# A new order of the work list in a fused attention and maxout kernel

## The chip, the cores and the metric

The kernel runs on one core of a Trainium2 chip. The metric is the device time of one execution in microseconds (us). The time before is the median of three runs, 335.35 us (334.3 to 336.46). The profile and the trace come from one profiled execution of the same kernel. Engines are called as in the profile: PE (matmul), PEld (its weight loads), DVE, ACT, POOL and SP.

## The reference

```python
# q, k, v: (8 batches, 12 heads, 448, 64) f32; w1, w2: (768, 1024); w_out: (1024, 768)
scores = scale * q @ k.T                    # scale = 1/8
scores = cap * tanh(scores / cap)           # cap = 30
attn = exp(scores - max) / (sum + 1e-9)     # softmax over the keys
x = (attn @ v)  -> transposed to (3584, 768)
h1 = x @ w1;  h2 = x @ w2
out = maximum(h1, h2) @ w_out               # (3584, 768) f32
```

## The kernel before, in words

**Algebra.** The maximum is written as relu(x @ (w1 - w2)) + x @ w2. So the kernel makes wd = w1 - w2 (step `sub`, six chunks) and wm = w2 @ w_out, which is premultiplied on chip (steps `W` and `WC` turn a chunk of w2 on PE and keep it, `OP` and `P` multiply it by w_out, `PC` keeps the result). Then out = relu(x @ wd) @ w_out + x @ wm. The tanh bounds the scores, so no maximum is subtracted.

**Attention.** The 96 (batch, head) pairs are worked in 24 quads t of four heads; a quad is two pairs i = 2t and 2t+1, and a batch has three quads. For a quad:

- `lk`, `lq` load k and q into one of two buffers `kqs` (POOL's DMA queue, L332 and L339; for pairs from 10 on the k load is two DMAs); `lv` loads v in four parts into `vp` and `vl` (L363, two buffers each).
- For pairs under 10 q and k are transposed on PE (`X`, `Xh`, L462) and kept by DVE (`XC`, `XCh`, L467). From quad 5 on one DMA transpose does it (`cr t`, L479, issued on SP), from `kqs` to one of two buffers `qkT`. So a load into `kqs` for quad t must wait for `cr` t-2, and `cr` t for the last scores of quad t-2.
- `S i j` makes the scores of a pair against 128 keys, for j = 0, 1, 2 (L517); `L t` those of the last 64 keys of all four heads (L531). They alternate between two PSUM slots `s0` and `s1`. ACT takes each with a tanh (`T`, L522; `TL`, L535), and exps follow in place (`E i j0 j1`, `EL`).
- `A` and `B` add the exps up on DVE (L551, L556), `Y` totals them over the keys on PE (L576), `Y1`, `Y2`, `Y3` transpose, invert and spread them (DVE, L581 to L587).
- `VL` and `V` make the values on PE, into one of the same two PSUM slots (L602, L610); `N t u` multiplies by the inverse and frees the slot (DVE, L622, L625). The result is x transposed, `xT`.

**Maxout.** 120 groups of matmuls, 30 for two batches: stage 1 (x @ wd, 448 columns) and stage 2 (relu part @ w_out and x @ wm, 384 columns). They run on four further PSUM banks. `M x y n` issues n pairs: one matmul on the upper 64 rows of the array for group x and one on the lower 64 rows for group y (L649; L644 where x is y). Where a group's bank passes from one half to the other, a hand-over nop carries the dependency: `Hs` on SP (L658), `H` on DVE. `ev` evicts a group on DVE (L670, L706, the last L709), `eva` on ACT (L704), `st` stores 192 KB of the output from SP (L680 to L685), the last two halves from SP and ACT (L711).

**What sets the order.** There is no scheduler at work: a text, `ORDER`, lists every step, and a loop at the end issues them as listed. Each engine (and each DMA queue, which is the issuing engine's own order) runs its instructions in list order; between engines only data, buffers and banks make them wait. `D` steps are matmuls on a constant that keep PE at work while it has nothing else.

```python
for s in ORDER.split(";"):
    if s.strip():
        name, *args = s.split()
        STEPS[name](*[int(a) if a.lstrip("-").isdigit() else a for a in args])
```

Of the kernel before, what the change touches and what calls it, by code (L numbers as in the profile page):

```python
# [9 lines left out]
ld0 k; ld0 q; ms0; lwo 0 0; dm; ms; D 3 27; lw2 2; lk 1 0; id; lq 1 0; cd k; cd q; lw2 0; Xh 0 0 0; lw2 3;  # L10
Xh 0 1; XCh 0 0; lw2 1; D 3 5; XCh 0 1; S 0 0; S 0 1; T 0 0; D 3 16; T 0 1; lq 2 0; S 0 2; D 3 17; lq 3 0;
T 0 2; lk 2 0; X 1 1; E 0 0 3; D 3 14; XC 1; lwo 0 1; L 0; D 3 20; TL 0; lk 3 0; W 3 2; D 3 2; lq 4 0; S 1 0;
WC 3; T 1 0; lv 0 0; W 1 3; EL 0; W 2 0; lv 0 1; WC 1; W 0 1; lv 0 2; WC 2; S 1 1; S 1 2; lv 0 3; T 1 1; WC 0;
X 2 2; lk 4 0; T 1 2; XC 2; OP 0 0 3; P 0 0 4; E 1 0 2; S 2 0; S 2 1; OP 2 0 0; P 2 0 2; lwo 1 0; P 2 0 2;
OP 1 0 1; P 1 0 2; T 2 0; P 1 0 1; lwo 1 1; X 3 2; T 2 1; lk 5 0; P 1 0 1; XC 3; S 2 2; lk 6 0; P 2 0 2; T 2 2;
P 2 0 2; lq 5 0; PC 2 0; E 1 2 3; L 1; lv 1 0; VL 0; V 0 0 0 2; lv 1 1; TL 1; X 4 2; lv 1 2; E 2 0 3;
V 0 1 0 2; XC 4; Y 0 0; V 0 0 2 3; V 0 1 2 3; Y1 0; lv 1 3; S 3 0; OP 2 1 2; P 2 1 1; Y2 0; P 2 1 2; T 3 0;
Y3 0; P 2 1 1; OP 1 1 0; P 1 1 3; N 0 0; P 1 1 1; EL 1; P 1 0 1; S 3 1; N 0 1; P 1 0 2; T 3 1; P 1 0 1; lw2 5;
PC 1 0; S 3 2; S 4 0; lk 7 0; T 3 2; OP 0 1 1; P 0 1 5; lw1 0; E 3 0 2; P 0 1 1; S 4 1; lw1 5; P 0 1 2;
P 0 0 2; PC 0 1; P 0 0 2; P 1 1 1; T 4 0; lq 6 0; P 1 1 1; PC 0 0; X 5 1; lw2 4; T 4 1; S 4 2; XC 5; P 1 1 2;  # L20
lv 2 0; T 4 2; OP 3 0 3; P 3 0 2; PC 1 1; W 5 1; lv 2 1; E 3 2 3; L 2; WC 5; VL 1; lv 2 2; V 1 0 0 2; TL 2;
V 1 1 0 2; Y 1 0; lv 2 3; sub 0 0; E 4 0 3; V 1 0 2 3; V 1 1 2 3; Y1 1; S 5 0; O 0 1; M 0 -1 1; lq 7 0;
P 3 0 2; Y2 1; P 2 1 1; Y3 1; lw1 2; P 2 1 2; T 5 0; X 6 0; lw1 1; N 1 0; P 2 1 1; EL 2; P 3 0 1; N 1 1; S 5 1;
sub 5 1; P 3 0 2; T 5 1; P 3 0 1; XC 6; S 5 2; PC 2 1; T 5 2; W 4 0; PC 3 0; S 6 0; E 5 0 2; WC 4; OP 3 1 2;
P 3 1 1; lk 8 0; X 7 3; lw1 4; S 6 1; XC 7; lq 8 0; P 3 1 2; T 6 0; P 3 1 1; sub 2 0; OP 4 0 0; P 4 0 1;
lk 9 0; P 4 0 3; T 6 1; lq 9 0; P 3 1 1; S 6 2; lq 10 0; P 3 1 2; T 6 2; sub 1 0; P 3 1 1; P 4 0 3; lw1 3;
P 4 0 1; E 5 2 3; L 3; PC 3 1; VL 2; V 2 0 0 2; TL 3; PC 4 0; V 2 1 0 2; lq 11 0; Y 2 3; sub 4 0; E 6 0 3;
lk 10 0; V 2 0 2 3; X 8 2; Y1 2; lk 10 1; V 2 1 2 3; XC 8; S 7 0; lk 11 0; X 9 0; Y2 2; T 7 0; Y3 2; lk 11 1;
M 0 -1 2; EL 3; N 2 0; OP 5 0 3; P 5 0 1; lv 3 0; S 7 1; P 5 0 1; N 2 1; P 5 0 1; T 7 1; P 5 0 1; OP 5 1 2;
P 5 1 1; lv 3 1; P 5 1 3; P 5 0 1; XC 9; lv 3 2; P 5 0 1; S 7 2; S 8 0; A 3 0 1; lv 3 3; T 7 2; P 5 0 2;  # L30
P 5 1 1; A 3 0 2; P 5 1 1; lv 4 0; P 5 1 1; E 7 0 2; P 5 1 1; PC 5 0; S 8 1; lv 4 1; OP 4 1 0; P 4 1 1; PC 5 1;
P 4 1 2; lv 4 2; P 4 1 1; sub 3 0; P 4 1 3; T 8 0; lv 4 3; P 4 1 1; A 3 1 1; lk 12 0; T 8 1; M 0 -1 1; S 8 2;
B 3 0; M 0 -1 1; lk 12 1; M 0 -1 1; T 8 2; O 1 3; M 1 -1 2; B 3 1; Hs 0; cr 5; M 1 -1 1; lq 12 0; M 1 0 1;
E 7 2 3; M 1 0 1; PC 4 1; M 1 0 1; O 2 2; M 2 0 1; L 4; lk 13 0; VL 3; A 3 1 2; TL 4; V 3 0 0 2; lk 13 1;
V 3 1 0 2; Y 3 0; E 8 0 3; V 3 0 2 3; lq 13 0; V 3 1 2 3; Y1 3; S 9 0; M 2 0 2; Y2 3; M 2 1 1; lv 5 0; Y3 3;
M 2 1 2; O 3 0; M 3 1 1; lv 5 1; M 3 1 1; ev 0; Hs 2; M 3 1 1; M 3 2 1; T 9 0; N 3 0; M 3 2 1; lv 5 2; M 3 2 1;
O 4 1; M 4 2 2; EL 4; Hs 3; ev 1; lv 5 3; M 4 2 1; S 9 1; M 4 3 1; N 3 1; lk 14 0; M 4 3 1; T 9 1; M 4 3 1;
O 5 3; M 5 3 2; Hs 4; lk 14 1; M 5 3 1; M 5 4 1; ev 2; M 5 4 1; S 9 2; lq 14 0; S 10 0; ev 3; M 5 4 1; T 9 2;
O 6 2; M 6 4 2; A 4 0 1; Hs 5; M 6 4 1; lk 15 0; M 6 5 1; E 9 0 2; M 6 5 1; ev 4; S 10 1; M 6 5 1; lk 15 1;
O 7 0; M 7 5 1; A 4 0 2; M 7 5 2; Hs 6; M 7 6 1; lq 15 0; M 7 6 1; ev 5; M 7 6 1; T 10 0; O 8 1; M 8 6 1;  # L40
A 4 1 1; M 8 6 1; Hs 7; M 8 6 1; cr 6; M 8 7 1; T 10 1; M 8 7 1; B 4 0; S 10 2; M 8 7 1; O 9 3; M 9 7 1; ev 6;
T 10 2; M 9 7 2; H 8; B 4 1; M 9 8 2; E 9 2 3; M 9 8 2; ev 7; L 5; VL 4; A 4 1 2; TL 5; V 4 0 0 2; V 4 1 0 2;
Y 4 2; E 10 0 3; V 4 0 2 3; V 4 1 2 3; Y1 4; S 11 0; lk 16 0; M 9 8 2; Y2 4; M 9 8 2; Y3 4; lv 6 0; M 9 8 3;
O 10 0; M 10 8 1; N 4 0; lv 6 1; M 10 8 1; Hs 9; M 10 8 1; T 11 0; M 10 9 1; N 4 1; M 10 9 1; Hs 8 2; lv 6 2;
M 10 9 1; M 8 9 2; EL 5; M 8 9 1; lv 6 3; S 11 1; M 8 9 2; A 5 0 1; M 8 9 1; T 11 1; lk 16 1; S 11 2; M 8 9 2;
A 5 0 2; O 11 2; M 11 9 1; lq 16 0; T 11 2; M 11 9 1; S 12 0; ev 8; M 11 9 1; M 11 10 2; ev 9; E 11 0 2;
M 11 10 1; lk 17 0; S 12 1; M 11 10 4; lk 17 1; M 11 10 4; T 12 0; lq 17 0; O 12 1; M 12 10 1; A 5 1 1;
M 12 10 1; Hs 11; cr 7; M 12 10 1; M 12 11 1; B 5 0; M 12 11 1; T 12 1; M 12 11 1; S 12 2; H 10 2; B 5 1;
M 10 11 1; T 12 2; M 10 11 5; E 11 2 3; st 0 0; M 10 11 2; O 13 3; M 13 11 1; ev 10; L 6; VL 5; A 5 1 2; TL 6;
V 5 0 0 2; V 5 1 0 2; Y 5 0; E 12 0 3; V 5 0 2 3; V 5 1 2 3; Y1 5; S 13 0; M 13 11 1; lv 7 0; M 13 11 1; Y2 5;  # L50
M 13 12 2; Y3 5; M 13 12 1; lv 7 1; M 13 12 3; N 5 0; M 13 12 1; lv 7 2; M 13 12 1; T 13 0; M 13 12 1; N 5 1;
M 13 12 1; lv 7 3; M 13 12 1; O 14 0; M 14 12 2; EL 6; Hs 13; S 13 1; lk 18 0; M 14 12 1; M 14 13 1; ev 11;
M 14 13 1; Hs 12 2; T 13 1; S 13 2; lk 18 1; M 14 13 1; A 6 0 1; M 12 13 2; T 13 2; Hs 14; M 12 13 1; lq 18 0;
A 6 0 2; S 14 0; M 12 13 3; E 13 0 2; M 12 13 1; S 14 1; lk 19 0; M 12 13 1; O 15 2; M 15 13 2; ev 12;
M 15 13 1; lk 19 1; M 15 14 2; ev 13; M 15 14 1; T 14 0; O 16 1; M 16 14 1; lq 19 0; A 6 1 1; M 16 14 1;
st 0 1; M 16 14 1; Hs 15; T 14 1; cr 8; B 6 0; M 16 15 1; S 14 2; M 16 15 1; ev 14; M 16 15 1; T 14 2; O 17 3;
M 17 15 2; H 16; M 17 15 1; B 6 1; M 17 16 2; E 13 2 3; M 17 16 1; ev 15; O 18 0; M 18 16 1; L 7; VL 6;
A 6 1 2; st 0 2; TL 7; V 6 0 0 2; V 6 1 0 2; Y 6 2; E 14 0 3; V 6 0 2 3; V 6 1 2 3; Y1 6; S 15 0; M 18 16 1;
lv 8 0; M 18 16 1; Y2 6; M 18 17 1; Y3 6; M 18 17 1; lv 8 1; M 18 17 1; O 19 2; M 19 17 2; ev 16; Hs 18;
lv 8 2; M 19 17 1; M 19 18 1; T 15 0; N 6 0; M 19 18 2; lv 8 3; O 20 1; M 20 18 2; EL 7; Hs 19; ev 17;  # L60
M 20 18 1; lk 20 0; S 15 1; M 20 19 1; N 6 1; M 20 19 1; T 15 1; M 20 19 1; lk 20 1; O 21 3; M 21 19 3; Hs 20;
M 21 20 1; lq 20 0; ev 18; M 21 20 1; S 15 2; S 16 0; ev 19; M 21 20 1; T 15 2; O 22 0; M 22 20 1; lk 21 0;
M 22 20 1; A 7 0 1; Hs 21; M 22 20 1; M 22 21 1; E 15 0 2; M 22 21 1; lk 21 1; ev 20; S 16 1; M 22 21 1;
O 23 2; M 23 21 1; A 7 0 2; M 23 21 1; Hs 22; lq 21 0; M 23 21 1; M 23 22 2; ev 21; M 23 22 1; T 16 0;
M 23 22 2; A 7 1 1; M 23 22 2; cr 9; M 23 22 1; T 16 1; M 23 22 1; B 7 0; S 16 2; M 23 22 2; B 7 1; O 24 1;
M 24 22 1; T 16 2; M 24 22 2; H 23; M 24 23 1; H 22 2; E 15 2 3; M 24 23 2; M 22 23 1; L 8; VL 7; A 7 1 2;
TL 8; V 7 0 0 2; V 7 1 0 2; Y 7 3; E 16 0 3; V 7 0 2 3; lk 22 0; V 7 1 2 3; Y1 7; S 17 0; M 22 23 1; lv 9 0;
M 22 23 1; Y2 7; M 22 23 2; Y3 7; M 22 23 1; lv 9 1; M 22 23 2; O 25 3; M 25 23 1; N 7 0; M 25 23 1; lv 9 2;
M 25 23 1; T 17 0; M 25 24 1; N 7 1; M 25 24 2; lv 9 3; M 25 24 2; EL 8; M 25 24 1; S 17 1; lk 22 1; M 25 24 2;
ev 22; M 25 24 1; T 17 1; S 17 2; lq 22 0; M 25 24 1; ev 23; M 25 24 1; O 26 0; M 26 24 1; T 17 2; M 26 24 1;  # L70
A 8 0 1; Hs 25; S 18 0; M 26 24 1; lk 23 0; M 26 25 1; A 8 0 2; M 26 25 1; Hs 24 2; E 17 0 2; M 26 25 1;
# [145 lines left out]
def kernel(  # L217
# [17 lines left out]
    B, H, S, D = q.shape  # L235
# [3 lines left out]
    P = 128  # L239
    KC, FC = DM // P, DF // P  # L240
    NP = H // 2
    N = B * NP
# [260 lines left out]
    expo = {}  # L503
# [15 lines left out]
    def tanh(i, j):  # L519
        if j == 0:  # L520
            expo[i] = att.tile([P, 2 * NJ, S], bf16, name=f"e{i % 2}")
        nc.scalar.activation(expo[i][:, 2 * j : 2 * j + 2, :], slots[i, j][:, :, :S], AF.Tanh, scale=scale / cap)  # L522
# [260 lines left out]
```

## Time and profile before

| what | before |
|---|---|
| time, median of 3 runs | 335.35 us (334.3 to 336.46) |
| span of the profiled execution | 332.5 us |
| instructions in the trace | 9803 |
| busy: PE, ACT, DVE, POOL | 321.8, 280.8, 240.4, 173.2 us |
| granted PE clock | 1.00 in every stretch |
| start of L602 (values tile) of quad 3, 11, 12, 23 | 60.6, 154.3, 165.7, 292.6 us |

The span is the time from the first to the last instruction of one execution; 2.85 us lie between it and the median of the runs. The busy time of an engine is what its instructions took; a PE that is busy is not therefore at its peak, since matmuls overlap. A row of a timeline gives start, length, engine, line, operation, what it writes and reads, and in brackets how long the engine had been idle and what ended that. The start of the first L602 of each quad is a good clock for progress, since there is one a quad.

### The profile page before, as it was taken

The page shows a single profiled execution, that of the slowest core. Times are in us where ns is not written, and L with a number is a line of the kernel's source. Part 1 is how long each engine was busy: PE and PEld are TensorE (multiplying, and loading weights), DVE is VectorE, ACT ScalarE, POOL GpSimd, SP SyncE. Part 2 cuts the span into 40 slices and gives each one's busy share as a digit, 9 for nine tenths or more (in the row PEclk, how much of TensorE's full clock was granted, in tenths as well). Part 3 has the DMA queues.
Part 4 walks back from the last instruction along what each step waited for, and adds up shares of the span by engine and source line. Part 5 has one row for each costly group of instructions (what it writes and reads, how often), then busy time and mean ns, then how long its engine had stood idle before and what let it go on. Part 6 is the DMA issues. An engine that isn't in the chain of part 4 may idle for free.

```text
span 332.5 us, 9803 instructions
## 1 busy us (share of the span) xinstructions
PE 321.8 (97%) x4139; PEld 183.9 (55%) x4140; DVE 240.4 (72%) x421; ACT 280.8 (84%) x276; POOL 173.2 (52%) x256
## 2 busy tenths in 40 slices
PE   7799998999999999999999999999999999999995
PEld 3444453455556655655656664556566556557662
DVE  2236879898788787986997788978888879973201
ACT  4799997999999999999999999999999999931120
POOL 6586698855775654746783582586456502000000
PEclk9999999999999999999999999999999999999999
DMA  7999999997999999999999999999997973013033
GB/s 137 190 155 184 231 229 135 104 141 71 162 194 188 83 209 140 166 100 164 173 175 95 164 169 170 141 92 194 177 139 71 225 168 45 3 49 97 0 97 95
DMA packets 136044, 45.89 MB, mean 138 GB/s; under 512 B 116417, under 2 KB 131009, under 8 KB 136001
## 3 DMA queue, kind: packets, MB, share of 16 engines
q0 software_dynamic: 96416, 25.08, 76.9%
q1 hardware_dynamic: 39280, 19.77, 30.6%
q8 instruction: 32, 0.52, 0.6%
q10 hardware_dynamic: 304, 0.43, 0.4%
q14 instruction: 12, 0.09, 0.1%
HBM read 47.45 MB, written 11.01 MB: 176 GB/s over the span
## 4 chain that ended last, share of the span: by engine, by line
PE 84%; DMA 8%; DVE 5%; issue 1%; POOL 1%; DVEq 0%; POOLq 0%
PE mm L649 60%; PE s L610 8%; PE s L517 8%; DMA osb<-in_moe_w_dram 2%; DMA gT<-in_moe_w_dram 2%; DMA xT<-in_moe_w_dram 2%; PE s L531 2%; DMA wo_sb<-in_moe_w_out_dram 2%; PE mm L576 2%; PE mm L644 1%; PE s L602 1%; DVE wd_sb L406 1%; PE mm L435 1%; DVE xT L625 1%; DVE wm_sb L441 1%
## 5 line engine op out<-in xcount | busy, mean ns | idle before, releaser
L522 ACT ACTIVATE e<-s 128x896 bf16<-128x896 f32 x144 | 125.5, 923 | 11.1 <-PE s L517 10.8
L539 ACT ACTIVATE e<-e 128x2688 bf16<-128x2688 bf16 (+2 forms) x72 | 122.6, 1704 | 0.0
L649 PE MATMUL mm<-wo_sb,gT 64*128 64x384 bf16 x864 | 115.1, 323 | 0.0
L649 PE MATMUL mm<-wm_sb,xT 64*128 64x384 bf16 x648 | 102.0, 322 | 0.0
L649 PE MATMUL mm<-xT,wd_sb 64*128 64x448 bf16 x768 | 96.7, 349 | 0.7 <-DVE wd_sb L406 0.6
L339 POOL DMA_DIRECT2D kqs<-in_k_dram x76 | 54.8, 723 | 63.8 <-DMA qkT<-kqs 63.2
L649 PEld LDWEIGHTS <-gT 64*128 64x128 bf16 x864 | 58.3, 94 | 25.7 <-issue 0.7
L649 PEld LDWEIGHTS <-wd_sb 64*128 64x128 bf16 x768 | 49.0, 94 | 26.9 <-DVE wd_sb L406 1.3
L649 PEld LDWEIGHTS <-xT 64*128 64x128 bf16 x648 | 50.6, 94 | 18.8
L517 PE MATMUL s<-qkT 64*128 64x448 bf16 x288 | 52.0, 353 | 2.0 <-DVE xT L625 1.7
L670 DVE TENSOR_SCALAR gT<-mm 128x448 bf16<-128x448 f32 x64 | 38.9, 618 | 8.8 <-PE mm L649 7.7
L363 POOL DMA_DIRECT2D vp<-in_v_dram x48 | 30.5, 642 | 22.0 <-PE s L517 21.5
L610 PE MATMUL s<-e,vp 128*32 128x448 bf16 x576 | 36.7, 354 | 0.0
L339 POOL DMA_DIRECT2D kqs<-in_q_dram x38 | 35.2, 926 | 1.0 <-DMA vp<-in_v_dram 1.0
L551 DVE TENSOR_TENSOR esum<-e 128x896 bf16<-128x896 bf16 x42 | 26.0, 619 | 9.7 <-ACT e L539 9.6
L363 POOL DMA_DIRECT2D vl<-in_v_dram x48 | 29.3, 617 | 5.9 <-DMA osb<-in_moe_w_dram 2.4
L517 PEld LDWEIGHTS <-qkT 64*128 64x128 bf16 x288 | 18.5, 94 | 23.1 <-issue 15.0
L625 DVE TENSOR_TENSOR xT<-s,inv 64x448 bf16<-64x448 f32 x48 | 29.9, 622 | 0.9
L551 DVE TENSOR_TENSOR esum<-esum,e 128x896 bf16<-128x896 bf16 x42 | 26.2, 624 | 5.8 <-ACT e L539 4.8
L704 ACT COPY osb<-mm 128x384 f32<-128x384 f32 x10 | 4.8, 479 | 26.9 <-PE mm L649 26.7
L706 DVE COPY osb<-mm 128x384 f32<-128x384 f32 x44 | 23.3, 553 | 5.1 <-PE mm L649 4.6
L556 DVE TENSOR_TENSOR esum<-esum,el 64x896 bf16<-64x896 bf16 x42 | 26.0, 619 | 1.2
(58 smaller groups left out, 266.6 us busy)
## 6 DMA issues: line engine op xcount, KB each, us to landing
out_dram<-osb SPq DMA_DIRECT2D x54, 192.0 KB, 4.8
vp<-in_v_dram POOLq DMA_DIRECT2D x38, 160.0 KB, 4.3
kqs<-in_q_dram POOLq DMA_DIRECT2D x47, 112.0 KB, 6.0
kqs<-in_k_dram POOLq DMA_DIRECT2D x76, 56.0 KB, 4.0
wo_sb<-in_moe_w_out_dram POOLq DMA_DIRECT2D x4, 384.0 KB, 6.6
osb<-in_moe_w_dram POOLq DMA_DIRECT2D x2, 512.0 KB, 5.6
osb<-in_moe_w_dram POOLq DMA_DIRECT2D x4, 256.0 KB, 6.6
kqs<-in_k_dram POOLq DMA_DIRECT2D x9, 112.0 KB, 6.6
```

The costliest lines, as they stand in the source:

```text
L339: nc.gpsimd.dma_start(out=to, in_=x)
L363: nc.gpsimd.dma_start(out=to, in_=x)
L517: nc.tensor.matmul(s[:, h, :S], k_of(t, o, h, j), q_of(t, o, h))
L522: nc.scalar.activation(expo[i][:, 2 * j : 2 * j + 2, :], slots[i, j][:, :, :S], AF.Tanh, scale=scale / cap)
L539: nc.scalar.activation(e, e, AF.Exp, scale=float(cap))
L551: nc.vector.tensor_add(d, e[:, 0:2, :] if j == 1 else d, e[:, 2 * j : 2 * j + 2, :])
L556: nc.vector.tensor_add(d, d, left_e[t][r, :, :])
L610: nc.tensor.matmul(vals[t][place(m, u), u, :S], w[:, m, :], expo[2 * t + o][:, 2 * j + h, :], start=False, stop=(j == NJ - 1))
L625: nc.vector.tensor_mul(x[r : r + 64], vals[t][r : r + 64, u, :S], sums[t, 3][64 - r : 128 - r])
L649: ins = nc.tensor.matmul(self.ps, w[r], x[r], start=first, stop=self.at == [self.n, self.n]).ins
L670: nc.vector.tensor_relu(gT[b // 2][:, f, cs], ps)
L706: nc.vector.tensor_copy(o[:, hs], ps)
```

## The change

The whole list is replaced by another one. Every kind of step occurs as often as before, with the same tiles and buffers, but for the hand-overs: 108 `Hs` and 23 `H` in place of 107 and 21. Runs of single `M` steps are joined (1985 entries in place of 2399). What moves:

- In front, w2's chunk 3 leads the POOL queue and w_out's first half comes behind four chunks of w2; the scores of a pair need not begin with j = 0 any more, which is what the edit in `tanh` allows.
- Loads are listed in bursts, in which those of two or three quads are mixed. Below, the loads and transposes of quads 15 to 17 are shown from both lists.
- `N` of a quad often stands behind two or three evictions on DVE; `Hs` stands directly behind `cr` in several places.
- At the end three stores stand together behind the last `eva`, and groups 118 and 119 alternate.

```diff
-ld0 k; ld0 q; ms0; lwo 0 0; dm; ms; D 3 27; lw2 2; lk 1 0; id; lq 1 0; cd k; cd q; lw2 0; Xh 0 0 0; lw2 3;
-Xh 0 1; XCh 0 0; lw2 1; D 3 5; XCh 0 1; S 0 0; S 0 1; T 0 0; D 3 16; T 0 1; lq 2 0; S 0 2; D 3 17; lq 3 0;
-T 0 2; lk 2 0; X 1 1; E 0 0 3; D 3 14; XC 1; lwo 0 1; L 0; D 3 20; TL 0; lk 3 0; W 3 2; D 3 2; lq 4 0; S 1 0;
...
-M 55 54 1; T 29 1; S 29 2; lq 34 0; M 55 54 1; ev 53; M 55 54 1; O 56 0; M 56 54 1; T 29 2; M 56 54 1;
-A 14 0 1; Hs 55; S 30 0; M 56 54 1; lk 35 0; M 56 55 1; A 14 0 2; M 56 55 1; Hs 54 2; E 29 0 2; M 56 55 1;
-S 30 1; lk 35 1; M 54 55 1; Hs 56; M 54 55 4; lq 35 0; M 54 55 3; T 30 0; O 57 1; M 57 55 1; A 14 1 1;
-M 57 55 1; cr 16; M 57 55 1; M 57 56 1; ev 54; M 57 56 1; T 30 1; M 57 56 1; S 30 2; ev 55; M 57 56 2; T 30 2;
...
-M 117 116 2; eva 115; M 117 116 5; st 7 4; M 117 116 4; M -1 116 2; Hs 117; M -1 116 1; M -1 117 2; Hs 116 2;
-M -1 117 1; M 116 117 8; M -1 117 2; eva 116; M -1 117 1; O 118 1; M 118 118 1; eva 117; M 118 118 6; st 7 5;
-M 118 118 7; O 119 3; M 119 119 2; ev 118; M 119 119 12; ev 119; st 7 6;
+ld0 k; ld0 q; dm; ms0; ms; cd k; id; lw2 3; lq 1 0; lk 1 0; lw2 0; lw2 2; lw2 1; lk 2 0; lq 2 0; lwo 0 0; lk 3 0;
+lq 3 0; lwo 0 1; D 3 8; cd q; D 3 24; Xh 0 0 0; Xh 0 1; D 3 4; XCh 0 0; XCh 0 1; D 3 4; S 0 1; D 3 4; W 3 2;
+S 0 0; X 1 1; T 0 1; T 0 0; WC 3; XC 1; S 0 2; L 0; D 3 28; W 2 0; D 3 4; T 0 2; E 0 0 3; TL 0; D 3 7; S 1 2;
...
+M 50 48 3; S 27 1; Hs 49; ev 47; N 12 0; ev 48; N 12 1; T 27 1; M 50 49 3; Hs 50; lk 30 0; lq 31 0; lq 30 0;
+lv 13 2; lk 32 1; lk 30 1; lv 13 0; lk 33 0; lk 31 0; lk 31 1; lv 13 3; lk 33 1; lv 14 3; lv 13 1; O 51 2;
...
+T 28 0; E 27 2 3; Hs 51; M 52 51 3; O 53 1; M 53 51 3; Hs 52; cr 15; A 13 0 2; ev 50; ev 51; M 53 52 3; S 28 1;
...
+ev 53; lv 15 3; lv 14 0; lq 33 0; lk 34 0; lv 14 1; lk 35 0; lq 35 0; lv 14 2; lq 32 0; lk 32 0; T 29 0;
...
+T 29 2; T 30 0; st 2 1; Hs 55; Hs 54 2; M 56 55 3; M 54 55 6; S 30 1; M 54 55 2; O 57 1; M 57 55 3; Hs 56; cr 16;
...
+Hs 116; st 6 2; M 114 115 6; O 117 2; M 117 115 2; eva 114; M 117 115 1; M 117 116 11; Hs 117; M -1 116 3;
+M -1 117 2; Hs 116 2; M -1 117 1; M 116 117 8; M -1 117 3; eva 115; eva 116; eva 117; st 7 4; st 7 5; st 7 3;
+O 118 1; M 118 118 4; O 119 3; M 119 119 4; M 118 118 10; M 119 119 6; ev 118; M 119 119 4; ev 119; st 7 6;
...
     def tanh(i, j):
-        if j == 0:
+        if i not in expo:
             expo[i] = att.tile([P, 2 * NJ, S], bf16, name=f"e{i % 2}")
         nc.scalar.activation(expo[i][:, 2 * j : 2 * j + 2, :], slots[i, j][:, :, :S], AF.Tanh, scale=scale / cap)
```

## The prediction

> **What bounds the kernel now.** First the page's busy shares, then its chain, then windows, then the timeline of one period. The columns of the windows are: time, sum, PE, PEld, DVE, ACT, POOL, granted clock, DMA share, GB/s.
>
> ```profile
> PE 321.8 (97%) x4139; PEld 183.9 (55%) x4140; DVE 240.4 (72%) x421; ACT 280.8 (84%) x276; POOL 173.2 (52%) x256
> ...
> 0.00:10.00 10.00, 7.33 (x51) 2.86 (x52) 1.84 (x9) 5.17 (x6) 6.00 (x15) 1.00 0.85 147
> 10.00:20.00 10.00, 8.72 (x125) 4.87 (x126) 3.83 (x6) 7.59 (x8) 6.42 (x12) 1.00 1.23 185
> ...
> 50.00:60.00 10.00, 8.62 (x80) 4.31 (x78) 9.69 (x18) 8.29 (x10) 8.53 (x13) 1.00 1.25 119
> 140.00:160.00 20.00, 20.00 (x276) 11.42 (x273) 16.41 (x30) 19.72 (x20) 12.31 (x19) 1.00 1.31 135
> ```
>
> The windows show two regimes. In the first 60 us PE is idle 6.7 us (the 10 us windows sum to 53.3 busy) and ACT some 12. From 60 to 320 PE has no gap, and ACT is at 19.0 to 19.9 of every 20 us until 280. The chain, in order of time (start, us, what), says the same:
>
> ```profile
> 1.26 6.20 DMA wo_sb<-in_moe_w_out_dram
> 7.75 7.10 DMA gT<-in_moe_w_dram
> ...
> 38.84 7.24 DMA osb<-in_moe_w_dram
> 46.07 0.81 issue
> 46.88 1.23 DVE wd_sb L406
> ...
> 323.81 4.67 PE mm L644 x28
> ```
>
> Until 58 us it runs through weight loads and DVE, then through PE alone to 328.5, an eviction and the last stores. One period (one quad of four heads, t) is what to price. In the timeline (start, us, engine, line), left-over scores L531 start at 154.12, their tanh L535 at 154.58, the values tile L602 at 154.32; the next L602 is at 165.73:
>
> ```profile
> 154.12 0.38 PE L531 MATMUL s<-qkT 64*32 64x448 bf16 x8
> 154.32 0.37 PE L602 MATMUL s<-el,vl 64*32 64x448 bf16 x8
> 154.58 0.92 ACT L535 ACTIVATE el<-s 128x896 bf16<-128x896 f32 x1 [0.22 <-PE s L531]
> 155.80 0.65 DVE L581 STREAM_TRANSPOSE st<-mm 128x448 f32<-128x448 f32 x1 [0.53 <-PE mm L576]
> ...
> 165.73 0.37 PE L602 MATMUL s<-el,vl 64*32 64x448 bf16 x8
> ```
>
> So a period is 11.41 us. Adding start-to-start times of its PE instructions (half-array pair of 384 columns 0.16, of 448 0.187, scores 0.19, four values 0.187, switches 0.20 to 0.30) gives 11.24. ACT's own sum is also 11.24: six tanh 0.80, exps 2 x 2.33 + 2 x 0.87, left-over tanh 0.82 less overlap, exp 0.84. **PE and ACT both fill the period; neither can wait for the other without loss.**
>
> Summing PE's start-to-start times over both lists between the values tiles of quads 3 and 23 gives 228.9 before (observed 232.0) and 228.0 after; both lists hold the same instructions of M, S, T, V and N. So the change can win only in the first 60 us and lose anywhere.
>
> **The change, part by part.** All sums are against the profiled execution: span 332.5, and 2.85 us around it to the median 335.35.
>
> 1. Front (before L602 of quad 3, now at 60.6). The first w2 chunk now leads the POOL queue, wo 0 0 goes behind four w2 chunks; sub, P and T are reordered. I walked both lists by the durations above. ACT falls 1.7 us behind near 20 us (two tanh stand behind a PE transpose unit that waits for w2), and wins 1.7 back where it idled 1.71 at 53.2. That puts quad 3's values tile at 60.4 instead of 60.6. Five more M steps and a sum stand ahead of it there: 1.75 us of PE work done early. Value -1.95. Bounds: ACT's work to that point is 47.5 us and starts no earlier than 6.65, so 54.2 against 59.5 is at best -5; a late w2 chunk (rows 7.1 to 7.5) can cost +2.
>
> 2. Steady state, order of DVE, PE and ACT. Each place where the new list takes a margin away is priced by its rows. Evictions (0.56 to 0.62) now stand ahead of N on DVE, and N (0.62 + 1.26, line below) frees the PSUM slot of the next scores: quads 6, 11, 12, 17, 18 are late by 0.17, 0.2, 0.35, 0.15, 0.25, sum 1.1. A scores pair directly before L602 needs 1.45 (0.46 to its tanh, 1.0 to the free slot): quads 5, 12, 13, 21 are short by 0.12, 0.25, 0.09, 0.13, sum 0.6. Scores j=1 before the first tanh is through: quads 5 and 13, 0.3 each. Totals behind sums (quad 14 to 15) and an H on DVE: 0.15 + 0.2. Value **+2.65**. Bounds: 0, if the observed 3.1 us over 20 periods (232.0 less 228.9) are the same margins and only change place; +5.5, if each late start also delays ACT's next exp by as much again.
>
> ```profile
> 158.17 1.26 DVE L625 TENSOR_TENSOR xT<-s,inv 64x448 bf16<-64x448 f32 x2
> 163.21 2.55 SPq L479 DMA_TRANSPOSE qkT<-kqs  x1
> ...
> 180.58 0.70 POOL L339 DMA_DIRECT2D kqs<-in_k_dram  x1 [5.57 <-DMA qkT<-kqs]
> ...
> qkT<-kqs SPq DMA_TRANSPOSE x19, 6.5
> kqs<-in_k_dram POOLq DMA_DIRECT2D x76, 56.0 KB, 4.0
> ```
>
> 3. POOL's loads and the DMA transposes (cr). kqs has two buffers, so a load for quad t waits until cr t-2 has landed, as 180.58 shows; behind it POOL's whole queue stands, and the trace has 63.2 us of such waits, harmless, for before each cr's last load stands behind no wait later than cr t-2. In the new list the loads of two or three quads are mixed: the last load for cr 7, 9, 12, 13, 15, 16, 18, 19, 21, 22 stands 2 to 7 issues behind one that waits for cr t-1. So cr t-1 and cr t form a chain: 6.5 (median landing) + 0.54 (POOL after it) + 0.72 per issue between + 4.0 (landing of the last k load). That is 15.4 for seven issues, 14.6 for six, 11.8 for two, against a period of 11.7. Slack to the first scores is 5.3 us (qkT free some 6.9 us after L602 of quad t-3; needed 7 us after that of t-2). Cr 14 to 15 to 16 (six, then seven) runs 2.9 + 3.7 = 6.6 late: a stall of 1.3. Cr 17 to 19 give 0.9 and up, cr 20 to 22 0 to 1.9, and one part of v for quad 7 stands behind cr 8's landing, 0 to 0.5. Hs 56, a hand-over nop on SP, stands behind cr 16 and shares its lateness. Value **+2.5**. Bounds: 0 with the quiet rows (k loads from 2.45, transposes from 4.2); with slow rows (transposes 7.5 to 8.4, loads 5.5 to 6.5) 6 us at cr 16 and some 10 in all.
>
> A rule speaks against this step. The Trainium skill's page "DMA: Bandwidth & Descriptors", section "Anatomy of one DMA — SWDGE (gpsimd) path", gives a GpSimd DMA as about 2.0 us plus its bytes by 436 GB/s: an estimate of 2.1 us for 56 KB. By that cr 16 would not stall and the time be some 336; the rows (median 4.0, quietest 2.45) stand between, and this sum uses the median.
>
> 4. Hs directly behind cr on SP (cr 5, 7, 8, 11, 13, 19, 22): cr holds SP 1.5 to 2.6 us, where before an H on DVE, or 4.5 us of PE work between, stood. Nothing of its own while cr starts on time, since Hs's bank turn is 3 us of PE work off; with a late cr it is in 3. Without that cover: 2 us each at worst, inside the upper bound of 3.
>
> 5. Tail: stores of 7 4, 7 5 and 7 3 all leave after the last ACT eviction, and groups 118 and 119 alternate. The last chain (PE, 0.56 eviction, 2.4 landing) is the same; the 192 KB stores (median 4.8) may run beside the last 96 KB ones. 0 to +0.5; value +0.3.
>
> 6. The tanh edit issues nothing. POOL's rows grow by 44 and are issue waits only: 0, hidden in POOL's 48% idle.
>
> Sum: -1.95 + 2.65 + 2.5 + 0.3 = +3.5; 336.0 in the profile's terms, 335.35 + 3.5 = 338.9, so **339**.
>
> **The rivals.** *Even* (334 to 337). Loads land as in quiet rows, margins absorb the order. For it: 63.2 us of POOL waits cost nothing before; instruction counts are the same. Against it: ten chained loads are new, and PE has no idle in which to lose. -1.95 + 0 to 2.65 + 0 + 0.3: 333.7 to 336.4.
>
> The Trainium skill's page "Perfetto Trace Analysis", section "Identifying the Most-Contended Engine", says that busy matmul time is no measure of PE's headroom. By it the gapless PE could hide idle that an order wins back; the row bounds that: 11.41 against 11.24, 0.17 x 20 = 3.4 us, and 332 in all.
>
> *The front really is shorter* (328.5 to 332). One mechanism: ACT's 12 us of idle in the first 60. If the first w2 chunk lands by 7 to 8 us instead of 14.85, the premultiplying units start earlier, fill PE between scores and ACT is fed without gap: up to -5 and the 1.75, giving 335.35 - 5 - 1.75 = 328.6, with step 2's 2.65 back 331.3. For it: the chain waits on wo at 1.26 to 7.46 and on that chunk to 14.85. Against it: the weights for the first subs leave POOL no earlier (about 52.5 for the last w1 chunk against 53.3), and keep DVE (9.69 of 10) full.
>
> *The chain of transposes binds at every place* (343 to 350): slow rows at all ten, +6 to +10 for step 3 and up to 5.5 for step 2: 335.35 - 1.95 + 0.3 + 10 + 5.5 = 349. For it: more loads in flight per burst, and landings lengthen with traffic (k 2.45 to 6.7). Against it: a late cr moves the loads behind it into quieter time.
>
> **How the numbers follow.** Forecast (337 to 343) 0.43; even 0.25; front shorter 0.15; chain binds 0.17. A change within 1% (3.35 us) is about what a measurement here can't tell from none. Faster by more than 1% (under 332.0) takes nearly all of the third: 0.14. Slower (over 338.7) takes the last and some 0.30 of the first: 0.47. The rest, 0.39. The range leaves out the ends of the outer cases, some 0.16: 331.5 to 347.
>
> **What would show it.** Right: L602 of quad 3 at 60.4 give or take 2; L602 to L602 of 11.6 in most periods, but a gap of 1 us or more ahead of L517 in quads 15 to 19, with releaser qkT; POOL's longest wait on qkT under 6.6, more in number. ACT busy below 19 of 20 in 170 to 220. Wrong: a PE without gaps from 60 on (then step 3 is 0); gaps in front of L517 with releaser DVE N larger than 0.4 (step 2 too small); a front that ends before 57 or after 63.

## The result

The new list is slower: 340.68 us against 335.9, as a ratio 1.0151 (95% interval 1.0114 to 1.0189), so about 5.1 us. (Runs of a kernel that fell in the chip's slower state are left out of the ratios, which is why a ratio need not be that of the medians.) The profiled execution has a span of 338.5 and took 340.31, so 1.8 us lie around a span, not 2.85: the profiled execution of before was one of its fastest, 1 us under its median.

Two windows of the old kernel, then the busy line of the page after the change and the same windows of the new kernel (columns as in the prediction):

```profile
100.00:120.00 20.00, 20.00 (x274) 12.43 (x274) 16.04 (x29) 19.14 (x20) 11.86 (x16) 1.00 1.29 141
...
200.00:220.00 20.00, 20.00 (x261) 10.74 (x257) 17.88 (x32) 19.22 (x20) 9.57 (x14) 1.00 1.19 132
```

```profile
PE 325.3 (96%) x4138; PEld 188.7 (56%) x4138; DVE 239.9 (71%) x421; ACT 285.1 (84%) x276; POOL 174.0 (51%) x256
...
100.00:120.00 20.00, 17.33 (x222) 10.02 (x220) 14.60 (x27) 17.78 (x18) 12.20 (x18) 1.00 1.20 129
200.00:220.00 20.00, 18.89 (x246) 10.68 (x247) 16.44 (x29) 18.16 (x18) 11.20 (x16) 1.00 1.44 188
```

PE had no gap between 60 and 320 before. Now it has 2.67 us of gaps in 100 to 120 and 1.11 in 200 to 220 (0.4 elsewhere), and ACT falls under 18.2 of 20 in the same two stretches.

The starts of the quads show where the 6.0 us between the spans arise:

| stretch | before | after | difference |
|---|---|---|---|
| start to L602 of quad 3 | 60.41 | 59.79 | -0.62 |
| quad 3 to quad 23 | 232.19 | 238.98 | +6.79 |
| quad 23 to the start of the last eviction | 35.91 | 35.30 | -0.61 |
| start of the last eviction to the end | 3.99 | 4.43 | +0.44 |

(L602 of the old kernel is L555 in the new one, the first instruction of each quad's values. In the fences below every line of the new kernel, and of the experiments on it, is 47 lower than in the old one; in e5 it is 6 lower. So L602 there is the old L649, a maxout pair, and L432 the old L479, the DMA transpose.) The sums of PE's start-to-start times are 228.9 and 228.0 for the second row. So the periods stand 3.3 us over their sums before and 11.0 after, 7.7 more; three periods hold 4.3 of it: 6 to 7 (13.78), 7 to 8 (13.51) and 15 to 16 (13.04).

The chain of the new kernel in order of time (start, us, what) in the worst of these:

```profile
92.45 0.95 PE mm L602 x10
93.40 0.15 PE s L484
93.55 7.74 DMA qkT<-kqs
...
101.82 0.70 POOL kqs L292
102.53 0.63 POOL vp L316
103.16 0.39 POOL kqs L292
...
103.86 0.71 POOL kqs L292
104.57 2.10 DMA vl<-in_v_dram
106.67 9.77 DMA qkT<-kqs
116.44 0.05 issue
116.49 0.36 PE s L470 x2
```

The transpose of quad 8 starts at 93.55. POOL waits for its landing with a k load of quad 10 (101.82); behind that stand a k load of quad 9 and two parts of v for quad 7. The k load of quad 9, issued at 103.15, landed at 106.40, and that ended SP's wait (the chain names a load of v behind it instead). The transpose of quad 9 can thus start only at 106.67, takes 9.77 us, and lands 0.05 us before its scores start. The timeline rows of POOL and PE (in brackets the idle time before and its end) give the same from the waiting side:

```profile
85.36 0.64 POOL L316 DMA_DIRECT2D vp<-in_v_dram  x1 [7.90 <-PE s L563]
101.82 0.70 POOL L292 DMA_DIRECT2D kqs<-in_k_dram  x1 [6.04 <-DMA qkT<-kqs]
...
116.49 0.36 PE L470 MATMUL s<-qkT 64*128 64x448 bf16 x2 [2.04 <-DMA qkT<-kqs]
...
208.75 0.55 PE L602 MATMUL mm<-xT,wd_sb 64*128 64x448 bf16 x4 [0.87 <-SPq L611]
```

The row at 85.36 shows why already the transpose of quad 8 was late: POOL stood 7.9 us with a part of v for quad 7, which needs the buffer of quad 5, ahead of quad 8's loads. The last row is a hand-over on SP that came late: SP had issued the transpose of quad 17 at 205.81 and two stores at 207.45 and 208.05 in front of it. The waits of SP (line, for what: us in total, times, longest), first before, then after:

```profile
SPq L479 <- PE mm L649: 24.4, 14, 2.6
SPq L479 <- PE s L517: 8.4, 4, 3.1
```

```profile
SPq L432 <- DMA kqs<-in_k_dram: 28.0, 10, 6.5
...
SPq L432 <- DMA kqs<-in_q_dram: 6.0, 5, 2.8
```

The old transposes waited for PE, and never for a load. Fifteen of the waits ahead of the new ones end with a load.

### The profile page after: what moved, and what is told of

Its sections match the earlier page's. It is cut to its first block, busy times and chain, and to the rows that moved or that the text cites. A ratio compares the mean times of both kernels' runs of the same rounds, so it can differ in the third digit from the quotient of the medians.

```text
span 338.5 us, 9785 instructions
## 1 busy us (share of the span) xinstructions
PE 325.3 (96%) x4138; PEld 188.7 (56%) x4138; DVE 239.9 (71%) x421; ACT 285.1 (84%) x276; POOL 174.0 (51%) x256
## 4 chain that ended last, share of the span: by engine, by line
PE 78%; DMA 10%; DVE 5%; issue 2%; SPq 1%; POOL 1%; ACT 1%; DVEq 0%; POOLq 0%
PE mm L602 52%; PE s L563 8%; PE s L470 7%; DMA qkT<-kqs 5%; PE mm L388 3%; DMA wo_sb<-in_moe_w_out_dram 3%; PE s L484 2%; DVE xT L578 2%; PE mm L529 2%; PE s L555 2%; PE mm L597 1%; DMA gT<-in_moe_w_dram 1%; SPq L638 1%; DVE wd_sb L359 1%; PE mm L415 1%
## 5 line engine op out<-in xcount | busy, mean ns | idle before, releaser
L475 ACT ACTIVATE e<-s 128x896 bf16<-128x896 f32 x144 | 127.0, 914 | 11.0 <-PE s L470 9.7
L492 ACT ACTIVATE e<-e 128x1792 bf16<-128x1792 bf16 (+2 forms) x72 | 121.8, 1696 | 0.6
L602 PE MATMUL mm<-wo_sb,gT 64*128 64x384 bf16 x864 | 113.2, 323 | 0.0
L602 PE MATMUL mm<-wm_sb,xT 64*128 64x384 bf16 x648 | 102.0, 323 | 0.4 <-SPq L611 0.4
L602 PE MATMUL mm<-xT,wd_sb 64*128 64x448 bf16 x768 | 99.9, 349 | 2.5 <-DVE wm_sb L394 1.6
L602 PEld LDWEIGHTS <-gT 64*128 64x128 bf16 x864 | 58.9, 94 | 25.2 <-issue 1.3
L602 PEld LDWEIGHTS <-wd_sb 64*128 64x128 bf16 x768 | 50.6, 94 | 29.0 <-issue 4.3
L602 PEld LDWEIGHTS <-xT 64*128 64x128 bf16 x648 | 49.4, 94 | 21.0 <-issue 2.1
L470 PE MATMUL s<-qkT 64*128 64x448 bf16 x288 | 55.4, 352 | 3.2 <-DMA qkT<-kqs 2.0
L316 POOL DMA_DIRECT2D vl<-in_v_dram x48 | 29.7, 621 | 30.0 <-PE s L555 29.0
L563 PE MATMUL s<-e,vp 128*32 128x448 bf16 x576 | 34.4, 354 | 0.0
L659 DVE COPY osb<-mm 128x384 f32<-128x384 f32 x44 | 24.0, 554 | 13.6 <-PE mm L602 13.2
L504 DVE TENSOR_TENSOR esum<-e 128x896 bf16<-128x896 bf16 x42 | 27.5, 663 | 7.5 <-ACT e L492 4.8
```

The source lines that it names most:

```text
L316: nc.gpsimd.dma_start(out=to, in_=x)
L470: nc.tensor.matmul(s[:, h, :S], k_of(t, o, h, j), q_of(t, o, h))
L492: nc.scalar.activation(e, e, AF.Exp, scale=float(cap))
L504: nc.vector.tensor_add(d, e[:, 0:2, :] if j == 1 else d, e[:, 2 * j : 2 * j + 2, :])
L563: nc.tensor.matmul(vals[t][place(m, u), u, :S], w[:, m, :], expo[2 * t + o][:, 2 * j + h, :], start=False, stop=(j == NJ - 1))
L602: ins = nc.tensor.matmul(self.ps, w[r], x[r], start=first, stop=self.at == [self.n, self.n]).ins
```

## The experiments

All are timed against the old kernel on the same chip, and all are edits of the list only: no work is left out. They ran on four chips, so it is the ratios that compare with one another; a point is 1% of the old kernel's time. Stretches of a trace come from one execution each.

**e1_loads_before.** The new list, with the loads of quads and values from the first DMA transpose on in the old order.

```diff
-...; lk 18 1; lk 19 0; lq 19 0; lk 18 0; lq 18 0; lk 20 0; lv 7 1; lk 19 1; lk 21 1; lv 7 2; lv 8 0; ...
+...; lv 7 0; lv 7 1; lv 7 2; lv 7 3; lk 18 0; lk 18 1; lq 18 0; lk 19 0; lk 19 1; lq 19 0; lv 8 0; ...
```

> The new list, but from the first DMA transpose on the q, k and v loads stand in the old order (each as early as its buffer allows); all else stays. Theory 'mixed loads': of what the periods lose in the changed kernel, 2.04 us stand before the first scores of quad 9, 0.63 before the values of quad 7 and 0.87 at a hand-over behind a late transpose of quad 17; all come from loads of later quads in front of needed ones, so this kernel takes 336.4 to 337.7, and no scores wait for a transpose. Rival 'small margins': the losses come from the order on DVE and PE and fill up what the loads leave; then it takes 339.5 or more.

Measured: 338.24, ratio 1.0088 (1.0054 to 1.0123), 0.6 points less than the new list and between the two expectations; the intervals overlap slightly. The gaps at quad 9 and at the values of quad 7 are gone; others came, of 1.42 us before the scores of quad 7, 1.13 at the hand-over after quad 17's transpose and 0.2 at quads 17 and 21. The loads are a cause, not the only one. A next suspect shows in SP's timeline of this kernel:

```profile
197.96 0.47 SPq L633 DMA_DIRECT2D out_dram<-osb  x1
198.48 0.60 SPq L634 DMA_DIRECT2D out_dram<-osb  x1
199.32 4.44 SPq L432 DMA_TRANSPOSE qkT<-kqs  x1
203.85 2.02 SPq L638 DMA_DIRECT2D out_dram<-osb  x2
```

A transpose that holds SP for 4.44 us (2.59 at most in the old kernel) directly behind two stores, and that landed 10.2 us after its start.

**e2_burst9.** Only the burst of quad 9 is mended.

```diff
-lk 18 1; lk 19 0; lq 19 0; lk 18 0; lq 18 0; lk 20 0; lv 7 1; lk 19 1; lk 21 1; lv 7 2; lv 8 0; lk 20 1; ...
+lk 18 1; lk 19 0; lq 19 0; lk 18 0; lq 18 0; lk 19 1; lv 7 1; lv 7 2; lk 20 0; lk 21 1; lv 8 0; lk 20 1; ...
```

> The new list, but in the one burst ahead of the transpose of quad 9 the k load of that quad and two parts of v for quad 7 are moved in front of the loads of quads 10 and of v for quad 8 that must wait for the transpose of quad 8. Mixed loads: the gaps of 2.04 and 0.63 go, 2.7 less, 338.0 give or take 0.5. Rival: the lateness only moves to the transposes after it, and the time stays within 1 us of 340.7.

Measured: 343.89, with runs from 337.0 to 347.0 and no ratio: inconclusive, for or against. In its profile the gap ahead of the scores of quad 9 is gone, and one of 2.62 us stands ahead of the values of quad 9, for a part of v.

**e3_front_after** and **e4_front_before.** Each takes one list up to the values of quad 3 and the other from there.

```diff
 ...; L 4; M 2 1 3;                     (new list so far)
-VL 3; Y 3 0; V 3 1 0 3; V 3 0 0 3; TL 4; ...
+...; cr 5; lq 12 0; lk 13 0; VL 3; TL 4; V 3 0 0 2; ...   (old list from here, less what is done)
```

> The new list up to the values tile of quad 3, and from there the old list (all steps not yet done, in its order). If the new front is worth what the trace shows (quad 3 at 59.8 in place of 60.4, and 1.75 us of PE work done ahead), it takes 333.0 to 334.5 against 335.9. Rival: ACT, which also fills the period, doesn't let PE use the work done ahead; then 335.3.

> The old list up to the values tile of quad 3, and then the new list. If front and steady state add up, 340.7 plus 0.6 to 2.4, so 341.3 to 343. Rival: the late transposes, not the front, set where the new steady state stands, and the time is that of the changed kernel, 340.7, within 0.5.

Measured: 334.6, ratio 0.9996 (0.9956 to 1.0036), for the new front with the old rest; 342.66, ratio 1.0211 (1.0171 to 1.0251), for the reverse. With the old rest, the periods are the old ones again (232.01 from quad 3 to 23 against 232.19), and the work done ahead buys nothing. With the new rest the old front costs 0.6 points (2.0 us) more than the new one, as expected if front and rest add up, though the intervals overlap. So the whole loss lies behind quad 3. The start of quad 3 itself moves between executions: 58.7 to 62.9 us in the eleven profiles with the new front. In six of them (e2, e3, e9, e10, e11, e13) PE was granted only half its clock for 3.4 us, between 56.7 and 61.7 us, and these are the six latest, 61.2 to 62.9; the other five lie at 58.7 to 60.7. In e3 itself it is 61.19, later than the 60.41 of the old kernel, so its trace could not have shown a gain.

**e5_old_new_loads.** The old list with the new order of loads.

```diff
-...; lv 7 2; lv 7 3; lk 18 0; lk 18 1; lq 18 0; lk 19 0; lk 19 1; lq 19 0; lv 8 0; ...
+...; lk 18 1; lk 19 0; lq 19 0; lk 18 0; lq 18 0; lk 20 0; lv 7 1; lk 19 1; lk 21 1; lv 7 2; lv 8 0; ...
```

> The old list, but from the first DMA transpose on its loads stand in the new order; all else stays. If the mixed loads alone make transposes late, whatever the rest: two or three gaps of 1 to 2.5 us ahead of scores or values, 337 to 339 against 334.9. Rival: only together with the new list's late stores and hand-overs do they cost; the old list's spare time of 1.5 to 5 us between a transpose's landing and the first scores takes them up, and the time stays at 334.9, within 1.

Measured: 345.75, ratio 1.0299 (1.0253 to 1.0345): the order of loads by itself costs twice what the whole change does. PE's waits in this kernel:

```profile
PE mm L643 <- SPq L652: 3.6, 2, 2.2
PE s L596 <- DMA vl<-in_v_dram: 1.8, 2, 1.4
...
PE s L604 <- DMA vp<-in_v_dram: 1.1, 1, 1.1
PE s L511 <- DMA qkT<-kqs: 1.0, 2, 0.6
```

Nearly half of these four comes through SP: hand-overs behind transposes that wait for loads. POOL stands here 29.5 and 25.4 us for buffers of v, next to 36.8 for transposes. One hand-over gap, of 2.16 us at 268.11, had 3.4 us at half clock right behind it; that period (quad 20 to 21) took 15.56 against 11.54.

**e6_n_first.** The new list with N directly behind the spread inverse, in 12 quads.

```diff
-Y1 12; ev 46; Y2 12; Y3 12; ...; ev 47; N 12 0; ev 48; N 12 1;
+Y1 12; ev 46; Y2 12; Y3 12; N 12 0; N 12 1; ...; ev 47; ev 48;
```

> The new list, but on DVE the two normalizing steps of each quad stand directly behind the spread inverse, ahead of evictions (11 quads change). Theory of step 2 (late N holds the next scores): 1.1 to 2 less than the changed kernel, 338.7 to 339.6, or a ratio of 1.009 to 1.012 to before; the periods of quads 6, 11, 12, 18, 19, 20, 21 end 0.2 to 0.4 sooner. Rival: the evictions that now come later hold the groups, and nothing is won or some lost: 340.5 to 342.

Measured: 347.17, ratio 1.0343 (1.0296 to 1.0389). Not won but lost, 6 us more than the new list: this part of the theory falls. How much of it is the edit's doing this run does not say, for its profile also has a late transpose at quad 9 (PE waits 2.9 us, against 2.04 in the new list) with 3.4 us at half clock behind it; e9 is the cleaner test.

**e8_loads_stores.** As e1, and five transposes ahead of the store that stood directly in front.

```diff
-Hs 58 2; M 60 59 3; M 58 59 2; Hs 60; st 3 3; cr 17; lk 38 0;
+Hs 58 2; M 60 59 3; M 58 59 2; Hs 60; cr 17; st 3 3; lk 38 0;
```

> The new list with the old order of loads, and besides that the transposes of quads 7, 8, 12, 13 and 17 stand ahead of the store that was directly in front of each on SP. With the old loads alone (338.2) those transposes held SP 3.7, 2.8, 2.6, 3.7 and 4.4 us and landed after 9.6, 8.4, 5.2, 9.2 and 10.2; gaps of 1.4, 1.1 and 0.2 stood behind them. If stores in flight cause that: under 2.7 on SP, under 8.5 to landing, gaps gone, 335.5 to 336.8. Rival: the loads in flight cause it, landings stay, 337.7 to 338.5.

Measured: 336.89, ratio 1.0039 (0.9999 to 1.0080), 0.5 points under e1, though the intervals overlap; the traces say it more clearly. The transposes of quads 7, 8, 12, 13 and 17 held SP 2.0, 1.7, 1.9, 2.1 and 3.3 us and landed after 7.4, 5.0, 4.6, 7.4 and 8.3, each shorter than in e1 (one held SP longer than the 2.7 expected); the one of quad 21, whose store was left in front, stayed at 4.2 and 10.2 (4.6 and 10.8 in e1). The windows of this kernel in the two bad stretches:

```profile
100.00:120.00 20.00, 20.00 (x274) 11.49 (x272) 15.93 (x30) 19.55 (x20) 9.90 (x14) 1.00 1.24 139
200.00:220.00 20.00, 19.94 (x262) 10.53 (x258) 17.41 (x32) 19.38 (x20) 9.61 (x14) 1.00 1.35 159
```

PE is full again. Quad 3 to 23 takes 235.06 (238.06 in e1): loads and stores together were 3.9 of the 7.7 us.

**e9_loads_stores_n.** e8 with the edit of e6.

> As the kernel with old loads and transposes ahead of the stores, and also with N ahead of the evictions. If the rest of the loss is the small margins, another 1 to 2 less, 334 to 335.5; what then remains over before would be the order of PE and ACT. Rival: no less than the kernel without it.

Measured: 344.14, ratio 1.0264 (1.0225 to 1.0302), 2.2 points over e8; quad 3 to 23 takes 241.14 against 235.06, with no half clock in it. The waits of PE say why:

```profile
PE mm L602 <- DVE gT L623: 5.4, 5, 1.7
```

The evictions that now stand behind N hold relu results that the second stage is waiting for. The new list's N behind evictions was the better order for it.

**e10_stores_only.** The new list and its own loads, with the edit on stores alone.

> The new list with its own loads, and only the transposes of quads 7, 8, 12, 13 and 17 put ahead of the store directly in front. With the old loads that was worth some 1.4 us (338.2 to 336.9). If a transpose's lateness here comes from waiting for k loads (28.0 us in 10 waits in the changed kernel), the order against the store matters little: 340 to 341, with the gap at quad 9 still there. Rival: stores are the larger part, 338.5 to 339.5.

Measured: 343.29, ratio 1.0233 (1.0181 to 1.0285). No gain. The trace shows no loss either: quad 3 to 23 takes 239.32 against 238.98 of the new list, and 1.8 of the 2.2 us between the two spans lie ahead of quad 3, where PE stood at half clock from 57.2 to 60.6. Its transposes wait 36.7 us for k loads (13 times); values wait 1.8 us for v and M pairs 1.5 us for hand-overs.

**e11_sorted_bursts.** The new list, each burst sorted by quad.

```diff
-lv 7 0; lv 6 1; lv 7 3; lq 17 0; lq 16 0; lk 17 0; lk 17 1; lk 16 1; lv 6 2;
+lq 17 0; lq 16 0; lk 17 0; lk 17 1; lk 16 1; lv 6 1; lv 6 2; lv 7 0; lv 7 3;
```

> The new list with its bursts of loads where they are, but within each burst those of the nearer quad first, so that no load needed for a transpose stands behind one that waits for the transpose before. If the mixing is the cause, most of what the old loads gave comes back: 338 to 339, no gap ahead of the scores of quad 9. Rival: the bursts themselves (late, and many in flight beside a transpose) are the cause, and 340 to 341 stays.

Measured: 345.15, ratio 1.0260 (1.0204 to 1.0315). That the mixing alone is the cause falls with this run. Its PE waits:

```profile
PE s L470 <- DMA qkT<-kqs: 6.3, 4, 3.1
```

Four late transposes (quads 7, 8, 13, 21), but none waited long for a load any more. Each started 0.3 to 0.4 us behind a store with 3 to 6 loads in flight, held SP 3.3 to 4.1 us and landed after 10.5 to 11.6. Behind the longest gap (3.14 us, quad 7) PE stood at half clock from 95.0 to 98.4, which is part of the price: quad 3 to 23 takes 243.20.

**e12_best.** e8, with the transposes of quads 10 and 21 also ahead of their stores, one store moved behind a hand-over, and six pairs of scores taken apart.

```diff
-O 27 2; M 27 25 3; st 1 3; Hs 26; cr 10;
+O 27 2; M 27 25 3; Hs 26; cr 10; st 1 3;
...
-M 74 73 1; S 37 1; S 37 2; M 74 73 2;
+M 74 73 1; S 37 1; M 74 73 2; S 37 2;
```

> Old loads, transposes ahead of stores (also those of quads 10 and 21, which held SP 3.1 and 4.2 us and were left in place before), one store moved from in front of a hand-over that PE waited 0.56 us for, and six pairs of scores taken apart by two pairs of matmuls. If what is left over the old list is the sum of such margins, 1 to 1.5 less than 336.9: 335.4 to 335.9, level with the old kernel. Rival: each gap closed opens one behind it, 336.5 or more.

Measured: 335.97, ratio 1.0010 (0.9974 to 1.0046): level with the old kernel, not under it, and not clear of e8 either. Nothing tried here beats both kernels.

**e13_sorted_stores.** e11 with the stores of seven transposes behind them.

> The new list with its bursts sorted by quad, and besides that the transposes of quads 7, 8, 10, 12, 13, 17 and 21 put ahead of the store directly in front. Sorting alone took 345.2, moving the stores alone 343.3, but with sorting the four transposes that scores waited for (quads 7, 8, 13, 21) all had a store end 0.3 to 0.4 us before them and loads in flight, held SP 3.3 to 4.1 us and landed after 10.5 to 11.6. If mixed loads and stores ahead hide each other, only both together help: 336 to 338, no landing over 9. Rival: the bursts themselves make the landings long, 340 or more.

Measured: 338.03, ratio 1.0057 (1.0026 to 1.0088). Sorting alone 1.0260, stores alone 1.0233, both 1.0057, neither 1.0151; quad 3 to 23 in the same order 243.20, 239.32, 235.63 and 238.98. Neither edit helps alone and both together do: the two faults hide each other. (The store edit is of seven transposes here and of five in e10.) Two of its transposes still landed late, after 10.0 and 10.6 us (quads 17 and 15), so the bound of 9 did not hold; the time is at the edge of what was expected.

## Why the prediction was right, point by point

The sign, the cause named as largest risk, and the size hold: +3.65 forecast against the median, 4.8 to 5.1 measured, inside the range. That the sum came so near is in part luck: steps 2 and 3 reached their sizes by other places and other terms than were counted.

1. **Front, -1.95.** The trace shows it: 0.62 at quad 3, and 0.9 and 0.85 less PE work in the two stretches after it by the sums of start-to-start times, 2.4 in all. In the new list e4 bears the size out: without the new front it takes 0.6 points, 2.0 us, more (the intervals overlap). e3 shows that it isn't money in hand: on the old rest it is worth 0 (within 0.4%). The step took PE work done ahead for time won; that ACT paces the period there is argued from its 19.0 to 19.9 of 20 us, not tried. It also left out a risk of its own: at 54 us the new front has PE wait 0.7 to 2.2 us for a part of wm (in eleven profiles), and in six of the eleven half the clock was lost for 3.4 us behind it.
2. **Order on DVE, PE and ACT, +2.65.** The size was near, its terms were not. e8, without the gaps of loads and stores, still has 3.75 us more over its sums than before. Adding up neighbouring PE instructions that start later than the same two usually do in the old kernel gives 4.65 us in e8 and 1.51 before: M behind M 1.76 (hand-overs behind stores, priced 0.2 with the rest), totals behind sums 1.56 against 0.68 (priced 0.15), scores behind scores 0.86 (priced 1.2 with those before L602), scores behind M 0.47 against 0.83. The last is the N term, priced 1.1, and it is no more than before: what failed is "quads 6, 11, 12, 17, 18 are late by ..." for N behind evictions, and e6 and e9 show that evictions first is the right way round.
3. **Loads and transposes, +2.5.** Under-sized if the stores are counted in: 1.0151 less 1.0039 is 3.8 us, 3.9 by the traces. The old loads alone (e1) take back 2.1 us by the ratios and 0.9 by quads 3 to 23; the rest came only with the stores moved, for which the step had no term. The chain of transpose, load behind a load that waits, next transpose is there as described, and so is the part of v for quad 7 (0.63 us; 0 to 0.5 was given). But it struck at quad 9, where the count gave three issues, and not at quad 16, which landed 3.2 us ahead of need. Two terms failed. The landing was taken as 6.5 everywhere; it was 3.4 to 9.8. And POOL's waits for v buffers (60.8 us, 21.5 before, against 29.7 for transposes) were not priced, though one of them made the transpose of quad 8 late. "Longest wait on qkT under 6.6, more in number" was wrong: 7.7, in 8 places.
4. **Hs behind cr, nothing of its own.** That held for transposes on time. The 0.87 us at quad 17 is the case named, a late transpose, with two stores beside it that the step didn't count; in all PE waited 1.3 us for such hand-overs, in three places, and for none before. That stores directly ahead lengthen the transpose itself was not foreseen at all.
5. **Tail, +0.3.** Measured 0.44 behind the last eviction.
6. **Tanh edit, 0.** Nothing in the trace speaks against it.
7. **Readings and signs.** Two readings were wrong without moving the sum. ACT's terms for a period as listed add up to 12.86 before any overlap, not 11.24: the rows hold one exp of 2.33 (from 155.39), one of 1.58 (from 160.96) and one short one, not two of each. And ACT's idle time in the first 60 us is 9.9 by the windows, not 12. Of the signs, quad 3 came as said (59.79), and ACT under 19 of 20 in 200 to 220; the gap of 1 us or more came at quad 9, not in 15 to 19, and the periods' median was 12.1, not 11.6.

The estimate of 2.1 us for a 56 KB load from the Trainium skill's page "DMA: Bandwidth & Descriptors" (section "Anatomy of one DMA — SWDGE (gpsimd) path") was the lower end here too: 2.38 at the quickest, 3.6 in the median of the whole run, 8.3 beside the transpose of quad 9. The rule of "Perfetto Trace Analysis" in the Trainium skill (section "Identifying the Most-Contended Engine") that busy matmul time is no measure of headroom agrees with these traces: the new periods stand 11.0 us over their sums, of which the windows from 60 to 320 show 4.2 as PE idle. A PE "without gaps" was therefore too weak a sign in the last part of the prediction.

The rival of a shorter front fell with the trace: the new front ends 0.62 us sooner, not several. The rival "even" fell with e5: the old list doesn't absorb the new loads. "Chain binds at every place" did not come for the change itself, but e5 (345.75) and e11 (345.15) are what it looks like.

## What to carry to other kernels

In a queue that waits in order, price every load by the slowest wait ahead of it, for each buffer that its neighbours need, and not only for its own. Keep a transpose on a shared queue away from stores directly ahead of it, and keep hand-overs from standing behind either. When two faults cover each other, undoing one alone looks like proof against it; try both together before dropping either. And before two profiles are compared, look at the granted clock stretch by stretch: a few microseconds at half clock in one of them can pass for the effect of an edit.

## What the runs showed of the hardware

The time of one and the same DMA transpose varied with what was in flight when it started. Over the 266 transposes in the profiles of the two lists and the twelve experiments:

| at its start | transposes | SP held, median (range), us | landing, median (range), us |
|---|---|---|---|
| no store within 0.5 us ahead, at most 1 load in flight | 36 | 1.48 (1.47 to 2.52) | 4.2 (3.4 to 6.8) |
| no store within 0.5 us ahead, 2 or 3 loads | 56 | 1.70 (1.47 to 3.28) | 5.2 (3.4 to 9.6) |
| no store within 0.5 us ahead, 4 loads or more | 142 | 2.07 (1.47 to 3.78) | 6.4 (3.4 to 11.3) |
| store ended within 0.5 us ahead, at most 3 loads | 12 | 1.80 (1.55 to 3.27) | 3.9 (3.5 to 10.5) |
| store ended within 0.5 us ahead, 4 loads or more | 20 | 3.64 (2.41 to 4.60) | 8.9 (4.4 to 11.6) |

The medians are long only where both come together, a store directly ahead and four loads or more; single long landings (up to 11.3 us) come without a store too. The edits of e8 and e13 show the part of the stores; that of the loads in flight is read from the counts alone and was not tried by itself.

The clock that PE was granted also fell, to half, for 3.4 us at a time: ten times between 30 and 320 us in the fourteen profiles (e2 and e11 twice; e3, e5, e6, e9, e10, e13 once; neither of the two lists). Two stretches of e11, at full and at half clock:

```profile
61.00:91.00 30.00, 30.00 (x394) 16.05 (x390) 23.97 (x43) 29.72 (x28) 18.11 (x26) 1.00 1.16 115
95.10:98.30 3.20, 3.20 (x22) 2.37 (x18) 3.04 (x6) 1.01 (x2) 3.00 (x5) 0.50 0.63 43
```

PE counts as busy in both, but at half clock it runs 22 instructions in 3.2 us, against 42 in as long a time at full clock (394 in 30 us). Each of the ten stretches began 0.3 to 2.1 us after the end of a gap of PE. All six gaps of more than 2.1 us were followed by one, and four of the sixteen gaps of 1.3 to 2.1 us. What decides between these was not tried. An estimate: 3.4 us at half clock lose 1.7 us of PE's work, so a gap of 2 to 3 us can cost well over what the gap alone shows.
